# A fused kernel with both halves rewritten: attention with token-major values and broadcast weighting, and a long convolution as a two-level Fourier transform shuffled through DRAM

## The chip, the cores and the metric

The kernel runs on one core of one Trainium2 chip. The metric is device time in microseconds (us), the median of several executions. "Before" took 497.24 us as first given (495.85 to 497.26, 3 runs). Two kernels are compared by the ratio of the mean time of one kernel's fast runs over that of the other's of the same rounds, so a ratio is not quite the ratio of the medians quoted. The experiments ran in other rounds than the changed kernel, on three chips (12, 13 and 3), and "before" alone moved by almost 3 us between them: a difference of 2 or 3 us between two medians is within that, and the intervals of the ratios decide.

The engines are called as in the profile: PE (TensorE, the matrix engine; PEld is its weight load), DVE (VectorE), ACT (ScalarE), POOL (GpSimd), SP (SyncE, which here only issues transfers).

## The reference

Two independent computations share one launch, and their results are put side by side in a 2048 x 1152 output.

```python
# A: sliding-window attention; S=2048, D=576, H=32 heads of Dh=18; 8 taps, 2 apart
q, k, v = split_heads(x @ wqkv)
logits[s, w] = q[s] . k[s - 2*w] * Dh**-0.5        # w = 0..7, masked where s - 2w < 0
o[s] = sum_w softmax(logits[s])[w] * v[s - 2*w]
a = o @ wo

# B: gated long convolution, every one of 576 channels on its own
kv = shift_conv_4taps(k, shift_k) * v
y  = irfft(rfft(pad(kv)) * rfft(pad(ssm_k)))[:S] + kv * ssm_D
b  = q * y
return concat([a, b], axis=-1)
```

The comparison takes both halves together, and with this input the attention half has a norm of 27.8 and the convolution half one of 0.00042 (computed from the reference). A wrong convolution cannot be seen in it. Each half alone: before has relative errors of 0.50% and 0.35%.

## The kernel before

Three parts matter; the listings here and below are shortened. First, the attention holds everything channel-major (partition = channel, 126 channels at a time). To weight v, PE copies each head's weight to its 18 channels (`ps_X`), ACT moves 90 of the 160 copies to SBUF, DVE multiplies tiles of 126 x 512, and PE adds the 8 taps with an identity matrix (`ps_oacc`).

```python
for ct, (c0, c1) in enumerate(CT):              # 5 channel tiles
    for j in range(NCH):                        # 4 x 512 tokens
        for w in range(W):                      # 8 taps
            nc.tensor.matmul(X[0:csz, :], Ej[0:NP, j, c0:c1], attn[0:NP, w, :], ...)      # ps_X
            if item % 16 < 9:
                nc.scalar.activation(Xs[0:csz, :], Xcur[0:csz, :], ACT.Copy)
                nc.vector.tensor_tensor(P[0:csz, :], Xs[0:csz, :], vsl, ALU.mult)
            else:
                nc.vector.tensor_tensor(P[0:csz, :], Xcur[0:csz, :], vsl, ALU.mult)
            nc.tensor.matmul(oacc[0:csz, :], ident[0:csz, 0:csz], P[0:csz, :], ...)       # ps_oacc
```

Second, the convolution is a dense Fourier transform of two halves of 1024 tokens with a sine table `TAB`: 1024 forward matmuls and 512 inverse ones, of 288 columns each.

```python
for tbb in range(NB):                           # 8 token blocks, for 8 frequency blocks, cos and sin
    for k, (d0, d1) in enumerate(DCH):
        nc.tensor.matmul(pss[k][:, 0:d1 - d0], TAB[:, tbb, cs, 128 * fb:128 * fb + 128],
                         src(tbb)[:, d0:d1], start=(tbb == 0), stop=(tbb == NB - 1))
```

Third, the program emits A, then B. The two halves overlap little.

## Time and profile before

| reading of before | value |
|---|---|
| span of the profiled run | 497.2 us |
| PE busy / DVE busy / ACT busy | 440.0 / 346.8 / 215.4 us |
| data moved | 27.45 MB |

The page of the kernel before begins so; each entry is busy us, share of the span, and instructions. Its part 2 cuts the span in 40 slices (digits are busy tenths).

```profile
span 497.2 us, 7433 instructions
...
PE 440.0 (88%) x2636; PEld 274.6 (55%) x2636; DVE 346.8 (70%) x917; ACT 215.4 (43%) x506; POOL 45.3 (9%) x84
...
PE   2889999999972698999299999899999999799996
...
DMA packets 20851, 27.45 MB, mean 55 GB/s; under 512 B 2359, under 2 KB 18879, under 8 KB 20814
```

Two stretches of the same kernel, in the view of busy times by window (start and end, length, busy time and instructions of each engine, granted PE clock, DMA share, GB/s):

```profile
112.00:150.00 38.00, 35.02 (x108) 9.62 (x108) 37.23 (x110) 4.14 (x8) 0.00 (x0) 0.98 0.00 1
...
345.00:420.00 75.00, 74.96 (x608) 59.38 (x608) 61.55 (x154) 26.30 (x75) 0.55 (x1) 1.00 0.04 11
```

The logits stage (112 to 150) is bound by DVE, the convolution (345 to 420) by PE, which never rests. The groups of instructions that the change removes (line, engine, operation, names, shape, count; busy us and mean ns; idle time before them):

```profile
L386 PEld LDWEIGHTS <-TAB 128*128 128x128 bf16 x960 | 93.8, 98 | 32.6 <-issue 9.1
...
L324 PE MATMUL ps_X<-attn,Ej 128*126 128x512 bf16 (+1 forms) x160 | 62.2, 395 | 7.4 <-ACT Xs L335 4.6
L340 PE MATMUL ps_oacc<-P,ident 126*126 126x512 bf16 (+1 forms) x160 | 61.1, 390 | 6.3 <-DVE P L336 5.7
L335 ACT ACTIVATE Xs<-ps_X 126x512 bf16<-126x512 f32 (+1 forms) x90 | 47.5, 615 | 22.1 <-PE ps_X L324 17.8
```

### The profile page before, as it was taken

The numbers are of one execution on the slowest core, as the hardware profiler recorded it, in microseconds if no ns is written. First come the engines' busy times: TensorE is split into PE (matmuls) and PEld (weight loads), VectorE is DVE, ScalarE is ACT, GpSimd is POOL, SyncE is SP. The second block draws the span as 40 slices with busy tenths as digits, with TensorE's granted clock in tenths as the row PEclk, the third lists the DMA queues.
The fourth block names the chain that finished last, engine by engine and source line by source line (L and its number), as shares of the span: only waits on it lengthen the run. The fifth ranks groups of instructions, "written<-read, shape, count | busy, mean of one in ns | idle before, by whom it ended". The sixth has DMA issues, their size and how long they took to land.

```text
span 497.2 us, 7433 instructions
## 1 busy us (share of the span) xinstructions
PE 440.0 (88%) x2636; PEld 274.6 (55%) x2636; DVE 346.8 (70%) x917; ACT 215.4 (43%) x506; POOL 45.3 (9%) x84
## 2 busy tenths in 40 slices
PE   2889999999972698999299999899999999799996
PEld 1455556322221344444145767667777776577775
DVE  2499810699995887888298029999369999983333
ACT  3589965200016477866366543233333333111111
POOL 9123000000000200001000011111000000011110
PEclk9999999999995699999689999999999999899999
DMA  8300050000000301000221226676000000022221
GB/s 258 104 3 0 1 142 1 1 0 1 1 0 0 102 1 48 2 0 13 84 60 36 99 94 203 184 218 194 1 2 1 1 1 1 1 73 73 84 84 36
DMA packets 20851, 27.45 MB, mean 55 GB/s; under 512 B 2359, under 2 KB 18879, under 8 KB 20814
## 3 DMA queue, kind: packets, MB, share of 16 engines
q1 hardware_dynamic: 11612, 12.40, 8.4%
q10 hardware_dynamic: 7298, 8.94, 5.7%
q0 software_dynamic: 1904, 5.65, 3.7%
q8 instruction: 20, 0.33, 0.3%
q14 instruction: 17, 0.14, 0.1%
HBM read 22.26 MB, written 4.72 MB: 54 GB/s over the span
## 4 chain that ended last, share of the span: by engine, by line
PE 57%; DVE 23%; ACT 11%; DMA 6%; issue 2%; ACTq 1%; DVEq 0%; SPq 0%
PE ps_log L282 11%; PE ps_proj L250 8%; PE ps_oacc L340 7%; PE ps_X L324 6%; PE ps_wo L357 4%; DMA kj<-in_B_k_dram 3%; DMA xnat<-in_A_x_dram 2%; ACT TAB L146 2%; ACT TAB L148 1%; PE ps_ktr L178 1%; ACT Xs L335 1%; PE ps_tr L238 1%; DVE Za_3162 L457 1%; DVE Zs_3164 L467 1%; DVE tA L421 1%
## 5 line engine op out<-in xcount | busy, mean ns | idle before, releaser
L386 PEld LDWEIGHTS <-TAB 128*128 128x128 bf16 x960 | 93.8, 98 | 32.6 <-issue 9.1
L324 PE MATMUL ps_X<-attn,Ej 128*126 128x512 bf16 (+1 forms) x160 | 62.2, 395 | 7.4 <-ACT Xs L335 4.6
L340 PE MATMUL ps_oacc<-P,ident 126*126 126x512 bf16 (+1 forms) x160 | 61.1, 390 | 6.3 <-DVE P L336 5.7
L335 ACT ACTIVATE Xs<-ps_X 126x512 bf16<-126x512 f32 (+1 forms) x90 | 47.5, 615 | 22.1 <-PE ps_X L324 17.8
L250 PEld LDWEIGHTS <-wq 128*126 128x126 bf16 (+1 forms) x300 | 39.4, 133 | 28.0 <-issue 3.5
L282 PE MATMUL ps_log<-prod,Eall 126*32 126x512 bf16 (+1 forms) x160 | 53.5, 377 | 0.6 <-ACT vTp_108 L262 0.6
L282 PEld LDWEIGHTS <-Eall 126*32 126x32 bf16 (+1 forms) x160 | 14.4, 93 | 39.4 <-issue 35.0
L324 PEld LDWEIGHTS <-Ej 128*126 128x126 bf16 (+1 forms) x160 | 21.7, 135 | 23.9 <-issue 15.0
L340 PEld LDWEIGHTS <-ident 126*126 126x126 bf16 (+1 forms) x160 | 21.3, 133 | 23.7 <-issue 14.2
L505 DVE TENSOR_TENSOR yb<-yb,mkd 128x288 bf16<-128x288 bf16 x32 | 9.7, 307 | 31.9 <-ACT yb L502 31.9
L178 PE MATMUL ps_ktr<-ident,knat 128*128 128x128 bf16 (+1 forms) x80 | 17.9, 224 | 15.4 <-ACT kT L184 10.9
L488 PEld LDWEIGHTS <-TAB 128*128 128x128 bf16 x256 | 25.8, 101 | 7.9 <-issue 0.7
L278 DVE TENSOR_TENSOR prod<-qT_94,kTp_99 126x512 bf16<-126x512 bf16 x32 | 13.2, 411 | 20.6 <-PE ps_proj L250 20.6
L496 PEld LDWEIGHTS <-TAB 128*128 128x128 bf16 x224 | 21.9, 98 | 8.0 <-issue 2.5
L284 ACT ACTIVATE Lsb<-ps_log 128x512 bf16<-128x512 f32 x8 | 4.8, 597 | 49.5 <-PE ps_log L282 49.5
L482 POOL DMA_DIRECT2D qt<-in_B_q_dram x16 | 8.7, 546 | 189.1 <-DVE stageB L506 92.4
L250 PE MATMUL ps_proj<-xT_133,wq 128*126 128x512 bf16 (+1 forms) x60 | 23.0, 386 | 1.9 <-ACT qT_95 L262 0.7
L184 ACT ACTIVATE kT<-ps_ktr 128x128 bf16<-128x128 bf16 (+1 forms) x60 | 16.3, 272 | 17.1 <-PE ps_ktr L178 17.1
L250 PE MATMUL ps_proj<-xT_137,wq 128*126 128x512 bf16 (+1 forms) x60 | 23.0, 383 | 0.0
L250 PE MATMUL ps_proj<-xT_136,wq 128*126 128x512 bf16 (+1 forms) x60 | 23.0, 383 | 0.0
L250 PE MATMUL ps_proj<-xT_134,wq 128*126 128x512 bf16 (+1 forms) x60 | 22.9, 385 | 0.0
L250 PE MATMUL ps_proj<-xT_135,wq 128*126 128x512 bf16 (+1 forms) x60 | 22.8, 383 | 0.0
(723 smaller groups left out, 1062.2 us busy)
## 6 DMA issues: line engine op xcount, KB each, us to landing
kj<-in_B_k_dram SPq DMA_DIRECT2D x31, 144.0 KB, 3.0
kj<-in_B_k_dram ACTq DMA_DIRECT2D x30, 144.0 KB, 2.9
vt<-in_B_v_dram POOLq DMA_DIRECT2D x16, 144.0 KB, 2.9
out_dram<-stageA SPq DMA_DIRECT2D x16, 144.0 KB, 1.7
qt<-in_B_q_dram POOLq DMA_DIRECT2D x16, 144.0 KB, 2.5
out_dram<-stageB SPq DMA_DIRECT2D x16, 144.0 KB, 1.8
wq<-in_A_wqkv_dram ACTq DMA_DIRECT2D x1, 1728.0 KB, 10.9
xnat<-in_A_x_dram SPq DMA_DIRECT2D x2, 576.0 KB, 7.3
```

The lines of the kernel that those rows point to most:

```text
L178: nc.tensor.transpose(ptr[:, 0:drows], knat[0:drows, db, 128 * lblk:128 * lblk + 128], ident[0:drows, 0:drows])
L184: nc.scalar.activation(dest, ptr[:, 0:drows], ACT.Copy)
L250: nc.tensor.matmul(ps[0:csz, :], wq[:, kb, comp * D + c0:comp * D + c1], xT[kb][:, 512 * j:512 * j + 512], start=(kb == 0), stop=(kb == 4),)
L278: nc.vector.tensor_tensor(prod[0:kp, :], qT[ct][0:kp, 512 * j:512 * j + 512], kTp[ct][0:kp, PADL - DIL * w + 512 * j:PADL - DIL * w + 512 ...
L282: nc.tensor.matmul(psw[32 * j:32 * j + 32, :], Eall[0:kp, ct, :], prod[0:kp, :], start=(ct == 0), stop=(ct == NCT - 1), tile_position=(0, ...
L324: nc.tensor.matmul(X[0:csz, :], Ej[0:NP, j, c0:c1], attn[0:NP, w, :], start=True, stop=True)
L335: nc.scalar.activation(Xs[0:csz, :], Xcur[0:csz, :], ACT.Copy)
L340: nc.tensor.matmul(oacc[0:csz, :], ident[0:csz, 0:csz], P[0:csz, :], start=(w == 0), stop=(w == W - 1))
L357: nc.tensor.matmul(pso[:, 0:dn], oT[ct][0:csz, 128 * sb:128 * sb + 128], wot[0:csz, ct, d0:d1], start=(ct == 0), stop=(ct == NCT - 1))
L386: nc.tensor.matmul(pss[k][:, 0:d1 - d0], lhsT, src(tbb)[:, d0:d1], start=(tbb == 0), stop=(tbb == NB - 1))
L488: nc.tensor.matmul(psos[k][:, 0:d1 - d0], lhsT, Za[g][:, fb, d0:d1], start=(fb == 0), stop=False)
L496: nc.tensor.matmul(psos[k][:, 0:d1 - d0], lhsT, Zs[g][:, fb, d0:d1], start=False, stop=(fb == NB - 1))
```

## The change

The intent is to remove most of PE's work in the convolution and in the weighting, and to run the halves together.

- Tokens are held as 128 x 16 (token = 16a + b, partition a). v is projected token-major with its columns permuted to (d, h), so one DVE multiply per 128 tokens weights all 8 taps and 576 channels, the weight broadcast over d. PE still sums the taps: 640 matmuls of 128 columns against the identity.
- The Fourier transform is done in two levels (a 128-point one over a, a small one over b). Between them data must change partitions, which goes through scratch arrays in DRAM: `Dk` (filter), `Dx` (kv), `Dy` (product), 4.7 MB each.
- Steps of A and B are interleaved by hand in the emitted program; a scheduler then orders each engine's queue by readiness within that.

```diff
-                            nc.tensor.matmul(X[0:csz, :], Ej[0:NP, j, c0:c1], attn[0:NP, w, :], ...)
-                                nc.scalar.activation(Xs[0:csz, :], Xcur[0:csz, :], ACT.Copy)
-                            nc.tensor.matmul(oacc[0:csz, :], ident[0:csz, 0:csz], P[0:csz, :], ...)
+            nc.vector.tensor_tensor(P[:].rearrange("p w (d h) -> p w d h", h=H), vs,
+                                    at[:, :, t2, :].unsqueeze(2).to_broadcast([128, W, DH, H]), ALU.mult)
+                        nc.tensor.matmul(oacc[0:csz, ci, 128 * u:128 * u + 128], Ps[u][:, wi, 128 * ct:128 * ct + csz], ident[:], ...)
... (start and first level)
+    nc.gpsimd.memset(vX[0:1, 0:14, :], 0.0)
+    permute_wv()                                    # GpSimd copy of the v weights
+    def k_step(c2): ...                             # filter: transposes, first level, store to Dk
+    def x_step(c2): ...                             # kv on DVE, first level, store to Dx
+    run(a_steps[0:12], [lambda c2=c2: k_step(c2) for c2 in range(8)])
+    run(a_steps[12:], [sk_step] + [lambda c2=c2: x_step(c2) for c2 in range(8)])
+    nc.sync.dma_start(vX[1:113, 0:14, :], vX[0:112, 16:30, :])       # v of the previous partition
... (one spectral group, 8 of them)
+    def g_step(g):
+        Wk, Wx = g_load(g)                          # from Dk and Dx
+        s2(Wk, g, Kc, 1.0 / 2048)                   # second level: PE, then ACT
+        s2(Wx, g, Xc, 1.0)
+        nc.vector.tensor_tensor(m1[:], Xc[:], Kc[:, 0]..., ALU.mult)    # and 3 more on DVE
+        ... inverse second level (PE), Y (ACT)
+        nc.scalar.dma_start(by_rt(Dy)[:, 4 * g:4 * g + 4, :], Y[:])
... (weighting and the last stage)
+    run([logit_step x8, softmax_step, at_step x4], [ia_tables, g_step 0..2])
+    run([pv_step 0..4], [g_step 3..7])              # pv_step: weighting and output of 2 x 128 tokens
+    run([pv_step 5..7], [y_step 0..7])              # y_step: load Dy and q, inverse first level, times q, store
```

## The prediction

> **What bounds the kernel now.** The page gives a span of 497.2 us with PE busy 440.0 us (88%), DVE 346.8, ACT 215.4. The chain that ended last: 57% PE, 23% DVE, 6% DMA. Busy times by stretch show three regimes: logits (112 to 150 us: DVE 37.2 of 38 us, 160 products starting 0.335 us apart); attention weighting (174 to 275: PE about 85%); and convolution (300 to 497, the largest block: PE 74.96 of 75 us from 345 to 420). The convolution is a dense 2048-point transform: 960+64 forward and 512 inverse matmuls of 288 columns, whose spacing on the timeline is about 0.122 us, so about 190 us. Removing matmuls there removes time.
>
> **What the change does.**
> Removed: 1536 transform matmuls (about 190 us PE), 160 expansion matmuls plus 160 512-column accumulations (about 70 us PE at 0.217 us), 90 Xs evictions (47.5 us ACT), 70 products from PSUM (43 us DVE), most of the sine table (24 us ACT).
> Added on PE: two-level transform: 102 first-level matmuls of 384 columns, 384 small second-level ones of 288, 64 inverse ones; 640 accumulations of 128 columns, each with its own weights; 66 transposes.
> Added on DMA: three scratch arrays of 4.7 MB written and read back, 28 MB, doubling traffic from 27 to about 54 MB. At 173 GB/s for a share of 0.57 (290 to 330 us) that is about 180 us of DMA, spread and prefetched.
>
> **Engine totals after** (estimates from trace durations):
> - PE about 260 us (220 to 290): transposes 10, v 21, k 19, q/k 41, x first level 8, logits 10 to 35, tables 9, second level 24 to 50, accumulation 52 to 70, output 21, inverse 8. The ranges ask whether matmuls on different column or row tiles overlap, as the Trainium skill ("TensorE: Matmul & The Clock Gate", Part 3) says, and what a 128-column matmul with fresh weights costs: the same page (Back-to-back issue gap) says about 81 ns; transposes in this trace run near 110 ns. Nothing in this trace shows tile overlap.
> - DVE about 200 us: kv 32x1.26=40, products 40, softmax 12, spectral products 31, weighting 16x2.46=39, rest 38. Slope from the trace: 128x512 bf16 0.335, 128x4096 2.29 us, a broadcast operand included, i.e. two elements a cycle.
> - ACT about 175 us plus 42 DMA issues.
>
> **Critical path by stage**: start until v projection about 21 us (x arrives at 12 us; GpSimd must finish a 1x8064 memset, about 7 us at 0.88 ns an element, before the weight permutation); v and k first level PE-bound to about 62; then DVE-bound: kv, products, softmax, three groups' spectral products, about 115 us, to about 182; at-transposes 6; weighting with five groups, PE-bound, about 65; the last three with the inverse about 37; output 4. Sum about 292 us.
>
> **Predicted: 292 us, 80% range 262 to 325.** Faster by over 2%: 0.98; within 2%: 0.01; slower: 0.01.
>
> **What would show each step right.** PE busy total near 260 to 290; matmul spacing of the accumulation 0.08 to 0.11 us; DVE 95% busy during products and softmax; weighting multiplies near 2.4 us; no long wait of second-level matmuls on scratch loads.
>
> **What would make it wrong.** Strided PE reads (transposes and v weights step 32 bytes, logits read runs of 8 bytes): if the PE slows on them, logits and v grow by 30 us or more. The weighting multiply dropping to one element a cycle: +39 us. Scratch loads blocked behind the 1.8 MB vX shift on the SP queue, stalling kv by 10 to 20 us. Stages overlapping better than my serial sum: 255.

## The result

The changed kernel takes 332.36 us (median of 4 runs, 331.76 to 332.86), before 497.25 us in the same rounds; the ratio is 0.6666 (95% interval 0.663 to 0.6702). The direction was right, the size was not: the time is 40 us over the forecast and 7 us outside its range.

The page of the changed kernel, the lines that answer to those shown of before, with the granted clock and the GB/s of each slice:

```profile
span 330.3 us, 5054 instructions
...
PE 241.9 (73%) x2125; PEld 153.7 (47%) x2129; DVE 210.3 (64%) x175; ACT 163.0 (49%) x236; POOL 36.9 (11%) x61
...
PE   2349999879997874385657166999998978876732
...
PEclk9987999999997997569858557799999999999965
...
GB/s 267 274 23 269 0 145 143 146 198 267 354 51 256 286 127 193 21 81 296 197 2 143 144 135 91 73 163 105 165 109 144 109 36 73 38 167 334 302 302 113
DMA packets 28355, 52.36 MB, mean 159 GB/s; under 512 B 2286, under 2 KB 22446, under 8 KB 28205
```

The totals came out as forecast: PE 241.9 us (forecast 220 to 290), DVE 210.3 (200), ACT 163.0 (175), 52.36 MB (54). So nothing costs more work than expected. No engine is now busy over three quarters of the span. The missing time lies between the instructions.

The view of windows of the changed kernel, cut at the borders of the stages:

```profile
27.00:71.00 44.00, 40.18 (x290) 32.98 (x290) 6.06 (x8) 27.34 (x39) 0.97 (x1) 0.97 0.37 128
71.00:88.00 17.00, 16.84 (x77) 7.73 (x79) 1.36 (x1) 7.82 (x9) 0.56 (x1) 1.00 0.97 292
88.00:127.00 39.00, 32.12 (x170) 14.54 (x170) 38.02 (x29) 24.26 (x30) 0.00 (x0) 0.96 0.57 193
127.00:140.00 13.00, 3.87 (x36) 1.23 (x39) 13.00 (x10) 1.07 (x2) 0.00 (x0) 0.55 0.36 106
140.00:178.00 38.00, 26.45 (x248) 10.23 (x243) 37.66 (x28) 17.42 (x28) 1.09 (x2) 0.75 0.42 141
...
205.00:290.00 85.00, 77.11 (x925) 55.06 (x925) 57.44 (x36) 53.78 (x89) 0.00 (x0) 0.98 0.30 99
290.00:330.00 40.00, 22.12 (x191) 15.23 (x188) 13.94 (x17) 5.08 (x8) 3.26 (x6) 0.83 0.79 252
```

From 88 to 178 the third number (DVE, after PE and PEld) nearly fills the window: the DVE-bound middle is as forecast. From 71 to 88 the transfers do (DMA share 0.97 at 292 GB/s) while DVE works 1.36 of 17 us. I compare borders of stages with the forecast, from the start times of the instructions that open them:

| border | forecast | measured |
|---|---|---|
| first v projection | 21 | 26.8 |
| first product of kv | 67 | 88.3 |
| first weighting multiply | 188 | 204.9 |
| last store of Dy | about 253 | 289.4 |
| end of the span | 292 | 330.3 |

(The forecasts are read from the prediction's sum: its DVE-bound middle of 115 us ends at 182, so it begins at 67; 6 us of transposes lead to 188, 65 of weighting with groups to 253. The sum does not close exactly: the stage before the middle ends at 62, and 188 + 65 + 37 + 4 is 294.) The 38.3 us over split into three: kv starts 21.3 us late; the middle takes 116.6 in place of 121, 4.4 less; and everything from the first weighting multiply to the end takes 125.4 in place of 104, 21.4 more. Nearly all of that lies before the last store of Dy: the weighting with five groups took 84.5 us (204.9 to 289.4) for 65, the last stage 40.9 for 41 (37 + 4).

The view of waits of the changed kernel (who waited, for whom: total us, times, longest):

```profile
DVE P L505 <- PE psA L514: 19.4, 6, 6.8
...
DVE skb L326 <- DMA tB<-in_B_shift_k_dram: 16.9, 1, 16.9
...
ACT Y L481 <- PE psB L478: 16.3, 9, 5.5
```

The middle line is DVE waiting for the load of the shift filter before kv. The other two belong to the weighting and the spectral groups: the multiply waits for PE to free its tile, the inverse's eviction waits for PE. The same view of the SP transfer queue alone:

```profile
SPq L360 <- DMA Dk<-vst: 32.8, 1, 32.8
...
SPq L360 <- ACT vX L220: 11.6, 1, 11.6
```

L360 is the shift of v, a copy within SBUF of 1.8 MB. Its turn in the queue was held up for 44.4 us: 32.8 are put by this view to stores to the filter's scratch array, 11.6 to the eviction of the last v projection, which ended at 72.07. It was issued at 72.1, in the very stretch where kv's loads should have landed, and the load of the shift filter (72.7) and those of k (73.5) stood behind it in the queue.

### The profile page after: what moved, and what is told of

It is laid out like the page before. It is cut to its first block, busy times and chain, and to the rows that moved or that the text cites. A ratio compares the mean times of both kernels' runs of the same rounds, so it can differ in the third digit from the quotient of the medians.

```text
span 330.3 us, 5054 instructions
## 1 busy us (share of the span) xinstructions
PE 241.9 (73%) x2125; PEld 153.7 (47%) x2129; DVE 210.3 (64%) x175; ACT 163.0 (49%) x236; POOL 36.9 (11%) x61
## 2 busy tenths in 40 slices
DMA packets 28355, 52.36 MB, mean 159 GB/s; under 512 B 2286, under 2 KB 22446, under 8 KB 28205
## 4 chain that ended last, share of the span: by engine, by line
issue 38%; DVE 26%; PE 15%; DMA 11%; ACT 4%; POOL 3%; SPq 1%; DVEq 0%; POOLq 0%
DVE prod L377 6%; PE psA L218 4%; DVE tB L343 4%; DVE tA L348 4%; DMA qt<-in_B_q_dram 3%; ACT vst L266 3%; PE psB L262 3%; DMA kX<-in_B_k_dram 3%; PE psB L285 2%; DVE n_132 L138 2%; DMA Wk<-Dy 2%; DVE W_73 L167 2%; DVE tA L343 2%; DVE stageB L543 2%; PE psA L202 1%
## 5 line engine op out<-in xcount | busy, mean ns | idle before, releaser
L505 DVE TENSOR_TENSOR P<-vX,at 128x4608 bf16<-128x4608 bf16 x16 | 40.3, 2554 | 20.6 <-PE psA L514 19.4
L514 PE MATMUL psA<-ident,P 128*128 128x128 bf16 (+1 forms) x640 | 46.3, 222 | 0.0
L266 ACT ACTIVATE vst<-psB 128x768 bf16<-128x768 f32 x48 | 36.6, 810 | 17.9 <-PE psB L262 17.3
L514 PEld LDWEIGHTS <-P 128*128 128x128 bf16 (+1 forms) x640 | 38.6, 101 | 9.7 <-issue 7.5
L231 PE MATMUL psA<-xT,wq 128*128 128x512 bf16 x156 | 37.1, 387 | 2.4 <-ACT vX L220 1.4
L527 PE MATMUL psA<-wot,oT 128*128 128x288 bf16 x160 | 22.8, 287 | 3.9 <-ACT oT L520 3.0
L218 PE MATMUL psA<-wv,xT 128*128 128x288 bf16 x160 | 24.2, 297 | 1.9 <-ACT vX L220 1.3
L435 ACT ACTIVATE Kc<-psB 128x576 bf16<-128x576 f32 x32 | 19.8, 649 | 6.4 <-PE psB L432 3.9
L218 PEld LDWEIGHTS <-xT 128*128 128x128 bf16 x160 | 20.4, 146 | 3.5 <-ACT xT L205 0.9
L377 DVE TENSOR_TENSOR prod<-q_0_83,k_0_85 128x4096 bf16<-128x4096 bf16 x8 | 18.3, 2284 | 0.3 <-PE psA L380 0.2
L377 DVE TENSOR_TENSOR prod<-q_1_84,k_1_86 128x4096 bf16<-128x4096 bf16 x8 | 18.2, 2281 | 0.0
```

The costliest lines, as they stand in the source:

```text
L218: nc.tensor.matmul(ps[:, di, 0:288], xTt[:, kb, t2, :], wv[:, kb, d0:d1], start=(kb == 0), stop=(kb == 4))
L231: nc.tensor.matmul(ps[:, u, :], wcols(kb, comp, ct), xT[:, kb, 512 * j:512 * j + 512], start=(kb == 0), stop=(kb == 4))
L266: nc.scalar.activation(vst[:, :, 384 * ch:384 * ch + 384], ps[:, :, 0:384], ACT.Copy)
L377: nc.vector.tensor_tensor(prod[:], q2[ct // 2][:], k2[ct // 2][:, :, sh:sh + S], ALU.mult)
L435: nc.scalar.activation(dst[:, :, prl, d0:d1], ps[:, :, 0:288], ACT.Copy, scale=scale)
L505: nc.vector.tensor_tensor(P[:].rearrange("p w (d h) -> p w d h", h=H), vs, at[:, :, t2, :].unsqueeze(2).to_broadcast([128, W, DH, H]), ALU ...
```

## The experiments

All are edits of the changed kernel.

### Shift of v later

```diff
-    nc.sync.dma_start(vX[1:113, 0:14, :], vX[0:112, 16:30, :])        # right after the kv steps
+    # pinned by the scheduler's order, after the loads of spectral group 0
+    run([logits, softmax, at], [ia_tables, lambda: g_step(0), shift_step] + [g_step 1, 2])
```

> The 1.8 MB copy of v rows inside SBUF is pinned behind the second pair of scratch loads on the SP queue instead of standing in front of the kv loads. Theory (transfers saturate and sit on the path between 72 and 88 us): about 2.0 MB leaves a window that moved about 300 GB/s, so the first kv multiply starts about 6 to 7 us after less waiting (near 82 instead of 88.3 us) and the total falls by 5 to 7 us, since the vector engine is 95% busy from there to the softmax. Rival (the start of kv is set by when the buffers of the first level come free and by issue, not by bytes): kv starts within 2 us of before and the total moves by under 2 us.

Measured: 325.42 us (324.42 to 327.39), ratio 0.6556 (0.6528 to 0.6584) against 0.6666 for the changed kernel. kv started at 77.8 in place of 88.3, weighting at 198.4 in place of 204.9. The transfer was on the path. But kv came 10.5 us earlier where the theory had said 6 to 7, and the run does not separate two things that moved together: 1.8 MB left the window, and the loads behind the shift had their turn sooner, the shift filter at 61.1 in place of 72.7, k at 70.6 in place of 73.5. The loads of k were held up by something else as well: in this run's view of waits their turn in the queue waits 9.0 us for the filter's last stores to Dk. By the code their buffers come from the memory that the filter's pool gives back; that this is the reason was not tested. A start 10.5 us earlier ended 7 us sooner. DVE's waits after its first product of kv were 1.4 us for k, 1.3 for a first-level matmul, and 5.0 in the softmax for ACT's exponential (2.3 in the changed kernel).

### Memset of the v row later

```diff
-    nc.gpsimd.memset(vX[0:1, 0:14, :], 0.0)
     permute_wv()
+    nc.gpsimd.memset(vX[0:1, 0:14, :], 0.0)
```

> The GpSimd memset of 1x8064 (6.8 us) is issued after the weight permutation instead of before. Theory (GpSimd work slows the vector engine: two 128x128 integer multiplies took 6.8 us together while it ran, later ones of 128x512 took 0.55 us): those two multiplies take under 1 us, transposed x is copied out earlier, the v projection starts 3 to 6 us earlier than 26.8 us, total down by 3 to 6 us. The 128x4096 table multiply (5.8 us) stays slow if GpSimd's copy still overlaps it. Rival (the multiplies are slow by themselves, e.g. for integers): they stay near 3.4 us each, no gain.

Measured: 339.22 us (338.18 to 340.96), ratio 0.6833 (0.6806 to 0.6859): slower. The mechanism was still shown. The timelines of the two kernels (start, length, engine, line, operation) first for the changed kernel:

```profile
4.76 6.84 POOL L191 MEMSET vX<- 1x8064 bf16 x1
4.94 6.81 DVE L138 TENSOR_SCALAR n_132<-g_130,p_f 128x128 int32<-128x128 int32 x2
...
15.63 5.34 POOL L294 COPY wv<-wq 128x2880 bf16<-128x2880 bf16 x1
...
17.33 5.80 DVE L167 TENSOR_TENSOR W_73<-C_154,lmask 128x4096 bf16<-128x4096 bf16 x1
```

and with the memset later:

```profile
4.93 0.53 DVE L138 TENSOR_SCALAR n<-g,p_f 128x128 int32<-128x128 int32 x2
...
19.07 6.81 POOL L297 MEMSET vX<- 1x8064 bf16 x1
19.15 6.84 DVE L180 CAST Eh<-e_f 128x192 bf16<-128x192 f32 x1 [8.76 <-POOL e_f L79]
...
26.25 2.28 DVE L167 TENSOR_TENSOR W<-C,lmask 128x4096 bf16<-128x4096 bf16 x1
```

The two integer multiplies took 6.81 us beside the GpSimd memset and 0.53 us without it; the table multiply 5.80 us beside the GpSimd copy and 2.28 without. Where the memset went, the little cast that met it took 6.84 us (0.24 in the changed kernel). The long DVE entries are not slow work: DVE stands still until GpSimd's instruction has ended (the memset ends at 11.60 and the multiplies at 11.75; the copy ends at 20.97 and the table multiply, with its own 2.2 us still to do, at 23.13). The Trainium skill, "SBUF — State Buffer", "Summary: rules for kernel authors", says so: against GpSimd some DVE forms fully block until the first to issue has finished. The run lost because a GpSimd instruction that DVE needs (`e_f`) was now queued behind the copy of the weights, and DVE stood 8.76 us before it. On top of that came the 6.84 us of the cast beside the memset in its new place, with the copies of transposed x behind it: v started at 32.8 in place of 26.8.

### The start repaired otherwise

```diff
-    nc.gpsimd.memset(vX[0:1, 0:14, :], 0.0)
+    nc.gpsimd.dma_start(vX[0:1, 0:14, :], xf[0:14, :])     # any finite rows: their weights are 0
-        nc.gpsimd.tensor_copy(wv[:]..., wq[...]...)
+        nc.scalar.activation(wv[:]..., wq[...]..., ACT.Copy)
```

> The GpSimd memset of 1x8064 is replaced by a small load of finite values (their weights are exactly 0), and the weight permutation moves to ScalarE behind the transposed x copies. Theory (a vector instruction that meets a GpSimd instruction of this kind waits until it has ended): the two integer multiplies take about 0.5 us together instead of 6.8, the table multiply 2.3 instead of 5.8, the first v matmul starts at 20 to 22 instead of 26.8 us and the total falls by 5 to 7 us. Rival (v cannot start earlier because x and the weights arrive late): start and total move by under 2 us.

Measured: 323.91 us (322.55 to 325.98), ratio 0.6496 (0.6453 to 0.6539). v started at 21.8, kv at 69.9: both near what I had forecast for the changed kernel (21 and 67). The later gain exceeds the 5 us of the start, because the queue order of SP changed with it: the loads of k were issued at 62.9, before the shift at 71.9. So this run removes both causes of the late kv, and is not the start alone. Of the 18.4 us gained at kv, 8.5 were left at the end. DVE waited 9.7 us for k's loads, but 7.8 of them before its first product of kv; after it, it waited 1.9 us for k, 0.9 for a first-level matmul and 4.6 for a q/k projection, 7.4 together.

### Filter transposes in the other PSUM pool

```diff
-        ptr = pb.tile([128, 2, 1024], BF16, name="psB")    # in k_step
+        ptr = pa.tile([128, 2, 1024], BF16, name="psA")
```

> The transposes of the filter take their PSUM tile from the other pool, so a filter step's four tiles no longer share two buffers. Theory (27 to 71 us is a serial chain of one filter step: 1.18 transposes, 0.77 copy, two evictions, 4.09 us a step): the step falls to 3.2 to 3.6 us, and kv and the total come 4 to 7 us earlier. Rival (bound by tensor engine work, 20.5 of 24 us busy from 47 to 71, or the other pool's two buffers now delay v): total within 2 us.

Measured: 331.97 us (330.58 to 334.2), ratio 0.6658 (0.6613 to 0.6703): no change, as its rival said. The eight filter steps, locked at 4.09 us in the changed kernel, now alternate between 4.2 and 5.8 us, presumably since they share two buffers with the projection. kv began at 78.2 (again a queue order: the loads of k came before the shift), but from there to 140 us DVE worked 52.0 of 62 us (in the changed kernel 51.0 of 52 after its kv start): after the first product its waits for k's loads (2.5 us), for first-level matmuls (2.0) and for a projection (4.6) took 9.1 of the 10 us back. An early kv start is worth only as much as its inputs are there.

### Only three weighting pairs beside the groups

```diff
-    run([pv_step 0..4], [g_step 3..7])
-    run([pv_step 5..7], [y_step 0..7])
+    run([pv_step 0..2], [g_step 3..7])
+    run([pv_step 3..7], [y_step 0..7])     # the first late multiply waits for the last group's product
```

> Only three of the eight weighting pairs may run beside the last five spectral groups; the first multiply of the other five is queued behind the last group's product. Theory (the inverse stage from 292.6 to 330.3 us is bound by transfers, about 9.5 MB at about 300 GB/s, while the tensor engine's cover for it had been used up earlier): the last scratch store lands 20 to 30 us earlier, transfers and weighting then overlap, the total falls by 15 to 30 us. Rival (tensor engine throughput over weighting, groups and inverse sets the sum of 204 to 330 us): the total moves by under 4 us, for the same work is only reordered.

Measured: 331.64 us (331.34 to 334.4), ratio 0.6689 (0.6659 to 0.6719): no gain, so the theory, as I had put it, fell. The last store of Dy came at 278.9 in place of 289.4, 10.5 us earlier where the theory had said 20 to 30, which the weighting left for the end ate up again. But the run showed what the groups are: the last ones, alone on the engines, took 12 and 13 us (their first products started at 246.95, 258.74 and 271.69). In one of them DVE stood idle 7.70 us before its product:

```profile
253.52 0.98 PE L432 MATMUL psB<-Wk,W 128*64 128x288 bf16 x8 [0.19 <-ACT Y L481]
...
254.54 1.82 ACT L435 ACTIVATE Kc<-psB 128x576 bf16<-128x576 f32 x3
...
256.34 2.37 ACT L435 ACTIVATE Xc<-psB 128x576 bf16<-128x576 f32 x4
...
258.74 1.36 DVE L468 TENSOR_TENSOR m<-Xc,Kc 128x2304 bf16<-128x2304 bf16 x1 [7.70 <-ACT Xc L435]
```

PE, ACT and DVE take turns. A group is a chain, and the next one begins only when it is over, although its data lie ready: the loads of this one were issued at 243.9 and 246.3 and took under 4 us, and its first matmul starts at 253.5.

### The spectral group pipelined by one

```diff
-    def g_step(g):
-        Wk, Wx = g_load(g)
-        s2(Wk, g, Kc, 1.0 / 2048); s2(Wx, g, Xc, 1.0)
+    def g_front(g):                      # load and second level
+        ...
+    def g_step(g):
+        if g == 0: g_front(0)
+        if g < 7: g_front(g + 1)         # before the product of g
+        Kc, Xc = kcs[g]
```

> New theory after the reordered weighting gained nothing: from 154 to 289 us the eight spectral groups are one serial chain, because the next group's second-level matmuls stand behind this group's product and inverse matmuls in the tensor engine's program order; with nothing else to do a group took 13 us there (258.7 to 271.7 us: about 5.5 us of evictions, 4.2 us of products with the tensor engine idle, 3 us of evictions), beside the weighting 12 to 18 us. Here the loads and second level of group g+1 are traced before the product of group g. Chain theory: the last scratch store is issued near 270 instead of 289 us and the total falls by 12 to 22 us. Rival (tensor engine work from 204 us on sets the end): under 4 us.

Measured: 316.80 us (315.55 to 317.5), ratio 0.6341 (0.6299 to 0.6384), 15.6 us less. Its windows from the first weighting to the last store of Dy, and from there:

```profile
205.00:272.00 67.00, 63.63 (x747) 45.43 (x746) 49.42 (x31) 45.38 (x75) 0.00 (x0) 0.93 0.25 87
272.00:316.00 44.00, 31.06 (x336) 24.86 (x333) 18.85 (x19) 8.08 (x12) 3.25 (x6) 0.93 0.75 236
```

DVE's wait of the weighting multiply for PE fell from 19.4 us (6 times) to 4.0 us (3 times) in the group stage. From the first weighting multiply (210.2) to the end (315.8) took 105.6 us; in the changed kernel 125.4; the forecast had 104. These three are not quite like for like: four of the eight groups' products now run before the first weighting multiply, three in the changed kernel, so the part holds one group less (PE busy 91.2 us for 99.2, ACT 49.3 for 59.0). Of the 19.8 us, 5.4 came back ahead of the weighting, which began at 210.2 in place of 204.9; 14.4 are left, about two thirds of the 21.4 us by which the part had been forecast too short. The sound measure is the whole kernel, 15.6 us less by an edit that removes no work from it, with the last store of Dy at 271.5 in place of 289.4. It also shows that PE's busy share misled. In the changed kernel's group window PE is busy 77.11 of 85 us, which looks bound by PE; over the whole of that part it is 99.2 of 125, and here 91.2 of 106.

### One load of Dy in the last stage (wrong)

```diff
-        nc.sync.dma_start(Vy[:, ri], by_f1(Dy)[:, ri, 2 * c2:2 * c2 + 2, :])
+        # only for c2 == 0; its block is used for all eight steps
```

> Wrong result on purpose: the inverse stage loads its first scratch block once and uses it for all eight steps, so 4.1 of about 9.5 MB leave the last stage. Theory (last stage bound by transfers): it shrinks from 37.7 us to 18 to 25 us and the total falls by 12 to 18 us. Rival (the chain of inverse matmuls, products and stores of one step after the other, two buffers each): under 4 us.

Measured: 323.62 us (322.38 to 324.27), ratio 0.6519 (0.6499 to 0.654): 9 us less; the last stage, from the first load of Dy to the end, took 28 us (292.8 to 320.7) in place of 37.7 (292.6 to 330.3). Between the two expectations: the loads of Dy are on the path, but they are not all of it; in what is left DVE waits 8.1 us for the loads of q and 5.3 for stores of the output.

### Four buffers for q

```diff
-        qt = b2.tile([128, 2, D], BF16, name="qt")
+        qt = b2.tile([128, 2, D], BF16, name="qt", bufs=4)
```

> Four instead of two buffers for q in the inverse stage, so two more blocks are loaded ahead of it. Theory (last stage bound by bytes): 0.59 of about 9.5 MB leave it, so 2 us at most. Rival (last stage bound by the round trip of a q load, 5.3 us from issue to landing with two buffers, issued only when a product has freed one): the steps of about 4.1 us shrink and the total falls by 4 to 9 us.

Measured: 329.73 us (328.63 to 330.01), ratio 0.6605 (0.6568 to 0.6642), 2.6 us less. The intervals overlap and the rounds differ, so this gain is not clear of noise: it is near what bytes alone would allow (2 us at most), and not the 4 to 9 us that hidden round trips would give.

### Four edits together

Late shift, repaired start, pipelined group and four q buffers.

> The changed kernel with four edits together: the shift of v late, the start repaired (no memset of the v row, permuting copy on ScalarE), the spectral group pipelined by one, and four q buffers. The separate gains were 7.0, 8.5, 15.6 and 2.6 us, sum 33.7. Theory (they lie on one serial sum, except that the first two both pull the first kv multiply forward, from 88 to 78 and to 70): 300 to 308 us, first kv multiply at 68 to 72, last store of Dy at 250 to 258. Rival (the time removed in one stage reappears as transfer contention in the next): 312 us or more, that is no better than the pipelined group alone (316.8) by over 2%.

Measured: 302.45 us (301.44 to 305.58), ratio 0.6084 (0.6041 to 0.6127), the fastest kernel. kv started at 72.2; the last store of Dy at 262.9, a few us later than I had expected. The total is inside the theory's range. The page of this run:

```profile
span 303.9 us, 5064 instructions
...
PE 241.2 (79%) x2129; PEld 155.4 (51%) x2129; DVE 200.6 (66%) x175; ACT 168.3 (55%) x237; POOL 24.5 (8%) x60
...
PE   2729998979997987669848354869999999995984
```

PE does the same 241 us of work in 26 us less. From the first weighting multiply (201.0) to the end took 102.9 us; the forecast had 104, but for five groups' products in that part, and here four are left for it.

### The same, with four blocks of Dy in flight

```diff
-        Vy = b2.tile([128, 4, D], BF16, name="Wk")
+        Vy = b2.tile([128, 4, D], BF16, name=("Wk", "Wx")[c2 % 2])    # both pairs of buffers are free by then
```

> As the run with the four edits, and the last stage loads its Dy blocks into both pairs of free buffers, so four blocks are in flight instead of two. Theory (the last stage waits for round trips of loads that start too late): 5 to 10 us less than the run with the four edits. Rival (it is bound by the bytes: 4.7 MB of Dy, 2.4 MB of q and 2.4 MB out at near 300 GB/s take 32 us): under 3 us less. The single-load run lay between such poles, so 3 to 5 would leave both in it.

Measured: 303.88 us (301.33 to 304.98), ratio 0.6109 (0.6076 to 0.6143): no gain, so the theory (round trips) falls; the rival (bytes) is left, by its number. Its windows:

```profile
265.00:285.00 20.00, 16.05 (x155) 12.04 (x153) 12.11 (x13) 3.28 (x6) 2.18 (x4) 0.91 0.95 305
285.00:299.60 14.60, 10.01 (x118) 8.24 (x115) 4.26 (x6) 2.97 (x5) 0.00 (x0) 0.99 0.52 180
```

While the loads run, the transfers are nearly full (share 0.95, 305 GB/s). Earlier loads only moved the same bytes forward: in the first 20 us from the first load of Dy on, the rate is 286 GB/s here and 254 in the run before, but from the last store of Dy to the end 244 and 238. After 285 us the transfers are at half (0.52, 180 GB/s) while pushed-back weighting pairs finish, so bytes alone do not bind the end of it. What binds it stays open.

### A alone and B alone (wrong, one run each)

```diff
-    run(a_steps[0:12], [k_step 0..7]) ...
+    run(a_steps[0:12], []) ...            # A alone; for B alone run([], [...]), without the shift of v
```

> The changed kernel with the convolution's steps left out (its half of the output is never written: wrong on purpose). If both halves had been made to overlap by the interleaving, A alone would cost near the whole. My sum from the changed kernel's durations: start 27, projections 34 at 0.217 us per 512-column matmul with the logits' products behind, logits 42, softmax 12, weighting 41, tail 8: 155 to 175 us.

> The changed kernel with the attention's steps left out (wrong on purpose). Theory (a chain of round trips through DRAM and of single spectral groups, which interleaving cannot shorten): start 20, filter 20 to 30, kv 45, groups 8 at 9 to 12 us, last stage 35 to 40: 190 to 235 us, with no engine busy over half of it. Rival (the conv is bound by its engines' work and only the interleaving stretches it): under 160 us.

Measured: A alone 225.48 us, B alone 284.04 us (single runs of unknown state). Both take far more than I expected: I was wrong by about 50 us over the upper end in each. PE's clock was granted low in both, in A alone at 0.50 to 0.67 from 90 to 172 us, so neither time is one at full clock, and neither is the sum that follows. The start of about 27 us is in both, and still: one after the other the new halves would take near the 497 us of before (an estimate: 225 + 284 - 27 = 482). Together they take 332. Of B alone, the page's span, engines and granted clock:

```profile
span 282.3 us, 2107 instructions
...
PE 137.0 (49%) x740; PEld 69.5 (25%) x740; DVE 118.4 (42%) x124; ACT 101.3 (36%) x151; POOL 36.9 (13%) x61
...
PEclk9995555555555555555755557557555765555755
```

and from its windows, the stretch of the spectral groups:

```profile
127.00:240.00 113.00, 63.99 (x426) 33.35 (x425) 35.38 (x37) 60.46 (x101) 1.08 (x2) 0.58 0.40 131
```

No engine is busy over half of the span: B is a chain of waits, as the theory said, though it took 49 us more than the theory allowed it. And over much of the span PE's clock is granted at half: the first-level matmul of 384 columns takes 0.524 us here (median) and 0.326 us in the changed kernel. The Trainium skill, "TensorE: Matmul & The Clock Gate", Part 1, describes a clock gate that idles at half rate; this trace shows that rate (0.50 over 33 to 127 us), though PE is busy 28.6 of the 39 us from 33 to 72, so which pauses bring it on no run here shows. A alone, on its side, leaves DVE idle all through its projections, as two of its windows show:

```profile
27.00:60.00 33.00, 33.00 (x211) 25.45 (x211) 0.00 (x0) 14.52 (x20) 0.00 (x0) 0.92 0.40 119
60.00:90.00 30.00, 28.33 (x156) 13.05 (x153) 1.57 (x1) 14.52 (x15) 0.00 (x0) 1.00 0.00 1
```

In the fused program kv and the filter fill that hole. What the single runs cannot tell is how much of B's 284 us is the slow clock and how much the chain; I have no run that holds the clock up without A.

## Why the prediction was wrong, and where it was right

Right, each by the trace of the changed kernel:

- The work removed and added. PE total, DVE total, ACT total and bytes all fell in or within 10% of the forecast.
- Tiles overlap. The Trainium skill, "TensorE: Matmul & The Clock Gate", Part 3, says that matmuls on different row or column groups run at the same time. Eight logits matmuls of 512 columns on four column groups took 0.64 us; one after the other, at the 0.217 us per 512 columns that the projections show, they would take 1.7.
- The accumulation with fresh weights came out below its forecast of 0.08 to 0.11 us, a miss that did no harm. One line of the timeline of the changed kernel shows 47 of them in 2.92 us; less 0.22 us for the last to finish, that is 0.059 us each:

```profile
234.32 2.92 PE L514 MATMUL psA<-ident,P 128*128 128x128 bf16 x47
```

- The broadcast multiply keeps the rate of the one before: 2.55 us for 128 x 4608, forecast 2.46 (the kernel before took 2.29 for 128 x 4096):

```profile
L505 DVE TENSOR_TENSOR P<-vX,at 128x4608 bf16<-128x4608 bf16 x16 | 40.3, 2554 | 20.6 <-PE psA L514 19.4 <-ACT at L422 1.2
```

- The middle is bound by DVE: 116.6 us from kv to weighting, of which DVE is busy 110.2, forecast 121.

Wrong was the step "Critical path by stage", in three terms:

1. "Weighting with five groups, PE-bound, about 65; the last three with the inverse about 37". Mis-sized by 21.4 us (with the output: 104 forecast, 125.4 measured), and nearly all of it in the first term: the weighting with five groups took 84.5 us for "about 65", the last stage 40.9 for 41. The step that failed is "PE-bound": the step took the stage to be bound by PE's work, and it was bound by the chain through PE, ACT, DVE, PE and ACT of one group at a time. Pipelining the groups by one took 15.6 us off the whole kernel without taking any work away, of which about 14 lie in this part. This cause is shown.
2. kv late by 21.3 us. The prediction had said of the transfers "spread and prefetched"; from 71 to 88 us they were neither, at a share of 0.97. Its last paragraph had named the culprit as a risk, the shift of v on the SP queue, with the right size of 10 to 20 us, but left it out of the sum. Moving the shift brought kv 10.5 us forward, repairing the start and with it the order of that queue 18.4. How much of this is bytes taken out of the window, and how much the turn of the loads in the queue, the runs do not separate; the loads of k came no sooner than 70.6 with the shift moved alone, because, as the view of waits puts it, their turn waited for the filter's last stores. What the first term of the sum, the start, missed (26.8 for 21) belongs here: it had counted the memset of GpSimd but not that DVE stands still while it runs.
3. The two errors do not add freely. An earlier kv met inputs that were not ready (after its start 1.4 to 2.5 us for k, 0.9 to 2.0 for first-level matmuls, and 4.6 for a projection in the two runs without the late shift), and gave back 3.5 to 10 us of what it had won (late shift 10.5 to 7, start 18.4 to 8.5, other pool 10 to none).

The four edits together end at 302, ten over the forecast, with the back half near its forecast length (102.9, with one group fewer in it than forecast) and the front half 13 us late at the first weighting multiply (201.0 for 188). I did not pursue these 13 us. Some 6 of them are likely the groups' fronts that now run ahead (with the start alone repaired, weighting began at 194.7); the waits of DVE that stand there are 9.7 us for k's loads (7.8 of them before kv starts) and 4.6 us for a projection.

What the prediction said least about carried most: the interleaving. By work alone the new halves look far lighter than the old ones (PE 242 us for 440); one after the other, by the estimate above, they would give nearly all of it back.

## What to carry to other kernels

Sum an engine's work to find what a change can gain, but draw the chain of one iteration through all engines before you call a stage bound by the busiest: a window with PE busy 91% still hid turn-taking that one reordering turned into some 15 us. Where a step is a chain, start the next one's front before this one's back. And a risk that you can name and size belongs in the sum: look at what else is in the queue ahead of the load that the next stage waits for.

## What the Trainium skill lacked or had wrong

- "TensorE: Matmul & The Clock Gate", "Back-to-back issue gap" gives about 81 ns for 128-column matmuls with fresh weights and about 131 ns for 512 columns. Here the former took 0.059 us (47 in 2.92 us) and the latter 0.217 us (160 projections in 34.7 us, A alone). What fits both is the page's formula for a single matmul's gap (56 and 216 ns), which this section says does not hold in a stream with weight loads; an earlier passage of the same page gives just these two as the spacing of warm matmuls back to back, so the page is not of one mind.
- "SBUF — State Buffer", "Summary: rules for kernel authors" has the blocking of DVE by GpSimd, and the trace agrees: a cast of 0.24 us took 6.84 us beside a memset on a single partition (1 x 8064). What no page that I read gives is how long such a memset takes: 6.84 us for 8064 elements, 0.85 ns an element.
- "DMA: Bandwidth & Descriptors", "Issuing engines are not separate DMA queues", treats the choice of issuing engine as a matter of the sequencer's time, usually small. Here the order within one issuing queue set the pace: the shift on SP, held for 44.4 us, stood before the loads of k, or behind them, or out of their way, and kv began at 88.3, or at 78 and earlier. Nothing there says that a transfer whose turn has to wait holds up all behind it.
- "SBUF — State Buffer" says in the same table to use about 358 GB/s for transfers between HBM and SBUF. The changed kernel moved 357 from 2 to 12 us, so the page agrees at best; other stretches with a share of 0.95 and 0.97 moved 305 and 292, and no run here shows what lowers it.
- No page that I read gives the cost of a permuting copy on ScalarE: 128 x 2880 elements with strided reads took 5.30 us, where an eviction of 128 x 1024 takes 1.02 (at that rate 2880 would take 2.9, an estimate).
